# A diffusion-transformer block: fewer dummy matmuls among the first modulation columns, two normalisations moved between scalings, and one K pair moved behind the second chunk's columns

## The chip, the cores and the metric

The kernel runs on one core of one Trainium2 chip. The metric is device time in microseconds (us) of one execution. A run is one execution; times of several runs are given as a median. The profile is one traced execution, whose own span (first to last instruction) is about 2 us shorter than the time.

## The reference

```python
B, N, D = (2, 256, 1152)
mod = (_silu(c) @ w_mod).reshape(B, 6, 1, D)
shift_a, scale_a, gate_a, shift_m, scale_m, gate_m = [mod[:, i] for i in range(6)]
h = _layernorm(x, axis=-1) * (1 + scale_a) + shift_a
qkv = (h @ wqkv).reshape(B, N, 3, H, Dh)
# ... attention, output projection, MLP (cut)
```

Only the opening matters here: layer norm of x, the modulation columns `scale_a` (a matrix-vector product with `w_mod`), the scaling, and the K projection of the scaled activations. (K is computed without `shift_a`, which only adds the same amount to all scores of a query.)

## The kernel before

The kernel writes its instructions down as units, and a small scheduler sets their order on each engine. TensorE (PE) keeps the written order; `S.first` fixes the first part of the order on DVE (VectorE) and ACT (ScalarE). The opening works like this:

- The four activation tiles (two per batch) are loaded, two at a time. DVE takes the statistics of tiles 1 and 2, ACT of tiles 0 and 3; GpSimd (POOL) raises the variance to the power -1/2, and DVE normalises (`xn_t`).
- TensorE transposes the normalised tiles (`xn_T`), and computes the scale columns in 2-column matmuls (`mod_kt`, 15 to a group), in two chunks: five of the nine column blocks first (`sca`), four later (`scb`). Each group of three K rows of `w_mod` is one load.
- DVE adds one to the columns (`sc1a`), DVE and ACT scale the transposed tiles (`hk_<row>_<batch>`), TensorE multiplies them with the K weights (`k_pair`).
- `warm(n)` issues n dummy matmuls of 512 columns, which nobody reads. They are there to keep the array's clock up.

```python
        def warm(n, tag):
            for i in range(n):
                S.unit("pe", 215.0, "warm_%s_%d" % (tag, i))
                mm(ps32(2), IDENT, Q4B, True, True)
...
        warm(12, "b")
        xn_T(1)
        warm(2, "c")
        for kt in range(0, 3):
            mod_kt(WSC, kt, 0, "sca_%d" % kt, (0, KC))      # group one
        xn_T(0)
        warm(2, "d")
        for kt in range(3, 6):
            mod_kt(WSC, kt, 0, "sca_%d" % kt, (0, KC))      # group two
        warm(3, "e")
        for kt in range(6, 9):
            mod_kt(WSC, kt, 0, "sca_%d" % kt, (0, KC))      # group three
        warm(3, "f")
        sc1a(0, KC)
        for kt in range(KC):
            hk(kt, 0, "act" if kt in (2, 4) else "dve")
        ...
        k_pair(range(KC), 0, 1)
        k_pair(range(KC), 1, 1)
        for kt in range(KT):
            mod_kt(WSC, kt, 0, "scb_%d" % kt, (KC, KT))     # chunk two's columns
        sc1a(KC, KT)
        for kt in range(KC, KT):
            for b in range(2):
                hk(kt, b)
        k_pair(range(KC), 2, 1)
```

## Time and profile before

Three runs took 250.62, 251.05 and 251.10 us, median 251.05 us.

The page of the kernel before, first its span and the busy times of part 1, then the engines' shares of the chain that ended last (part 4):

```profile
span 248.7 us, 4155 instructions
PE 242.5 (98%) x1831; PEld 149.8 (60%) x1831; DVE 69.9 (28%) x179; ACT 63.8 (26%) x129; POOL 19.7 (8%) x33
...
PE 94%; ACT 2%; DMA 1%; DVE 1%; issue 0%
```

TensorE is busy nearly all the time and makes up nearly all of the chain. So the question for each part of the change is how much earlier TensorE gets through the opening. The chain of waits of the kernel before, in order of time (start, length, engine and line; line 722 is the statistics, 744 the normalisation, 681 the transposes, 678 all other matmuls, 774 the addition of one, 783 the scaling, 874 a memset of half a query tile):

```profile
...
7.38 0.47 DVE arena L722
7.84 0.49 DVE arena L744
8.33 0.05 issue
8.38 0.68 PE psum L681 x9
9.06 0.81 PE psum L678 x17
9.87 0.52 PE psum L681 x9
10.39 2.00 PE psum L678 x35
12.39 0.02 issue
12.42 0.18 DVE arena L774
...
12.62 0.36 DVE arena L783
...
13.03 1.92 PE psum L678 x16
...
16.83 5.40 PE psum L678 x75
22.23 0.16 DVE arena L774
22.38 0.11 issue
22.49 0.28 DVE arena L874
...
22.80 0.30 DVE arena L783
...
23.14 38.59 PE psum L678 x312
...
```

Read it from the top. Tile 1's normalisation (7.84) releases the first transposes (8.38). From there to 12.39 TensorE never waits: transposes, columns and dummies follow each other. The addition and the first scaling (12.42 to 12.98) release K at 13.03. At 22.23 the chain leaves TensorE again for DVE: addition, memset, first scaling of chunk two. TensorE stood 0.31 us there; chunk two's K starts at 23.14.

A summary of the opening, from successive starts of matmuls in the trace and from its landing records (when the last of 16 engines reported a load):

| before | us |
|---|---|
| first activation tiles landed (x) | 4.37 |
| first transposes | 8.38 |
| group one: weights landed / started | 8.45 / 9.32 |
| group two | 9.71 / 10.66 |
| group three (m): weights landed / started | 10.99 / 11.71 |
| K of batch 0 started | 13.03 |
| chunk two's K started | 23.14 |

### The profile page before, as it was taken

Reading aid. Unit: us, or ns where it says so; the run is one execution under the profiler, and the core shown is the slowest. Engines: PE = TensorE matmul, PEld = TensorE weight load, DVE = VectorE, ACT = ScalarE, POOL = GpSimd, SP = SyncE. Lnnn points to the kernel's source line nnn. Section 1 sums busy time; section 2 is a strip of 40 time slices with the busy share of each in tenths; the row PEclk is TensorE's granted clock in tenths of the full one; section 3 lists DMA queues with packets and bytes.
Section 4 is the critical chain, followed back from the end, with each engine's and each line's share of the span. In section 5 each row is a group of like instructions: output and inputs, shape, how many; then the busy total and the mean of one; then the engine's idle time right before and its main releaser. Section 6 shows DMA issues by size and latency. Waiting matters only on the chain.

```text
span 248.7 us, 4155 instructions
## 1 busy us (share of the span) xinstructions
PE 242.5 (98%) x1831; PEld 149.8 (60%) x1831; DVE 69.9 (28%) x179; ACT 63.8 (26%) x129; POOL 19.7 (8%) x33
## 2 busy tenths in 40 slices
PE   7799999999999999999999999999999999999995
PEld 2588864557656856698644444444556665666574
DVE  3543350456412768951000000000011222211112
ACT  5630340334311402985323322233000000000000
POOL 1400000000003258510000000000000000000000
PEclk9999999999999999999999999999999999999999
DMA  6999969999999999999955660000000000000000
GB/s 246 364 375 391 391 216 409 427 419 420 417 388 354 264 367 390 391 392 383 365 171 175 190 188 4 0 0 0 3 16 16 18 16 16 16 18 17 31 18 17
DMA packets 27644, 51.59 MB, mean 207 GB/s; under 512 B 1511, under 2 KB 15591, under 8 KB 26475
## 3 DMA queue, kind: packets, MB, share of 16 engines
q1 hardware_dynamic: 27216, 50.14, 55.7%
q0 software_dynamic: 384, 1.19, 1.5%
q8 instruction: 14, 0.23, 0.4%
q14 instruction: 3, 0.02, 0.0%
q10 hardware_dynamic: 27, 0.00, 0.0%
HBM read 50.14 MB, written 1.19 MB: 206 GB/s over the span
## 4 chain that ended last, share of the span: by engine, by line
PE 94%; ACT 2%; DMA 1%; DVE 1%; issue 0%
PE psum L678 91%; PE psum L681 2%; DMA arena<-in_x_dram 1%; ACT arena L1051 1%; ACT arena L1035 1%; ACT arena L730 1%; ACT arena L731 1%; DVE arena L783 0%; DVE arena L744 0%; DVE arena L722 0%; DVE arena L774 0%; DVE arena L874 0%; DVE arena L1141 0%; DVE arena L732 0%; DVE arena L1142 0%
## 5 line engine op out<-in xcount | busy, mean ns | idle before, releaser
L678 PE MATMUL psum<-arena 128*128 128x384 bf16 (+7 forms) x1724 | 238.7, 306 | 1.7 <-POOL arena L701 1.4
L678 PEld LDWEIGHTS psum<-arena 128*128 128x128 bf16 (+1 forms) x1724 | 144.0, 97 | 91.6 <-issue 3.0
L1141 DVE TENSOR_TENSOR arena<-psum,arena 128x384 f32<-128x384 f32 (+3 forms) x14 | 7.0, 501 | 119.1 <-PE psum L678 119.1
L1061 ACT ACTIVATE arena<-psum 128x512 bf16<-128x512 f32 (+1 forms) x44 | 22.5, 522 | 42.6 <-PE psum L678 42.6
L673 ACT ACTIVATE arena<-psum 128x512 bf16<-128x512 f32 (+7 forms) x29 | 15.4, 553 | 37.3 <-PE psum L678 33.8
L675 DVE CAST arena<-psum 128x512 bf16<-128x512 f32 (+4 forms) x23 | 14.0, 621 | 30.9 <-PE psum L678 30.8
L1030 POOL TENSOR_TENSOR arena<-arena 128x384 f32<-128x384 f32 x12 | 10.9, 911 | 11.2 <-DVE arena L1029 10.1
L722 DVE BATCH_NORM_STATS2 arena<-arena 128x6 f32<-128x384 f32 (+1 forms) x18 | 9.5, 549 | 1.1 <-DMA arena<-in_x_dram 1.0
L681 PE MATMUL psum<-arena 128*128 128x128 bf16 (+2 forms) x107 | 7.8, 209 | 1.5 <-DVE arena L744 1.4
L681 PEld LDWEIGHTS psum<-arena 128*128 128x128 bf16 (+2 forms) x107 | 6.3, 97 | 4.2 <-DVE arena L744 1.9
L1035 ACT ACTIVATE arena<-arena 128x1152 bf16<-128x1152 f32 x4 | 5.4, 1354 | 9.5 <-DVE arena L1034 9.5
L1029 DVE TENSOR_TENSOR arena<-psum,arena 128x384 f32<-128x384 f32 x12 | 6.6, 548 | 3.2 <-PE psum L678 3.2
L1142 DVE TENSOR_TENSOR arena<-arena 128x384 bf16<-128x384 f32 (+3 forms) x14 | 7.0, 501 | 0.5
L1051 ACT ACTIVATE arena<-psum,arena 128x128 bf16<-128x128 bf16 x16 | 6.1, 460 | 3.2 <-PE psum L681 2.5
L659 POOL DMA_DIRECT2D dit_scratch<-arena x2 | 1.2, 628 | 62.9 <-DVE arena L675 62.9
L1048 DVE TENSOR_SCALAR arena<-psum,arena 128x128 bf16<-128x128 bf16 x20 | 5.5, 336 | 2.0 <-PE psum L681 1.8
L926 ACT ACTIVATE arena<-psum,arena 128x256 bf16<-128x256 f32 x8 | 3.7, 470 | 6.9 <-PE psum L678 5.4
L726 POOL TENSOR_TENSOR arena<-arena 128x1 f32<-128x1 f32 x6 | 3.3, 551 | 8.3 <-DVE arena L725 8.3
L889 ACT ACTIVATE arena<-arena 128x256 bf16<-128x256 bf16 x6 | 2.5, 495 | 4.3 <-DVE arena L883 4.3
L783 DVE TENSOR_SCALAR arena<-psum,arena 128x256 bf16<-128x256 bf16 x7 | 2.3, 348 | 3.6 <-PE psum L681 2.3
L922 DVE TENSOR_REDUCE arena<-psum 128x2 f32<-128x512 f32 x4 | 2.8, 690 | 1.5 <-PE psum L678 1.5
L930 DVE TENSOR_TENSOR arena<-arena 128x512 bf16<-128x512 bf16 x4 | 2.8, 688 | 0.1
(37 smaller groups left out, 31.0 us busy)
## 6 DMA issues: line engine op xcount, KB each, us to landing
arena<-in_w_mod_dram SPq DMA_DIRECT2D x3, 3456.0 KB, 26.2
arena<-in_w_fc_dram SPq DMA_DIRECT2D x9, 1152.0 KB, 9.9
arena<-in_w_fc_dram SPq DMA_DIRECT2D x4, 2592.0 KB, 20.5
arena<-in_wqkv_dram SPq DMA_DIRECT2D x18, 288.0 KB, 9.0
arena<-in_w_mod_dram SPq DMA_DIRECT2D x3, 864.0 KB, 12.6
arena<-in_wqkv_dram SPq DMA_DIRECT2D x1, 2592.0 KB, 9.8
arena<-in_wo_dram SPq DMA_DIRECT2D x1, 2592.0 KB, 40.1
arena<-in_w_mod_dram SPq DMA_DIRECT2D x3, 480.0 KB, 7.6
```

The lines of the kernel that those rows point to most:

```text
L673: act(c_act(n), lambda e: e.activation(out=dst, in_=src, func=ACTF.Copy), [src], [dst], name)
L675: dve(c_dve_psum16(n) if psum16 else c_dve_psum32(n), lambda e: e.tensor_copy(dst, src), [src], [dst], name)
L678: S.instr(lambda e: e.matmul(o, lhsT=l, rhs=r, start=st, stop=sp, **kw), reads=[l, r], writes=[o])
L681: S.instr(lambda e: e.transpose(o, i_, idn), reads=[i_, idn], writes=[o])
L722: dve(550, lambda e, s=s, o=o: e.bn_stats(out=o, in_=s), [s], [o], "bn_%s_%d" % (tag, ci))
L1029: dve(550, lambda e, o=o, ga=ga, x1c=x1c: e.tensor_tensor(out=x1c, in0=o, in1=ga, op=ALU.mult), [o, ga], [x1c], "wo_t1_%d_%d" % (t, ci))
L1030: S.op("pool", 930, lambda e, xs=xs, x1c=x1c: e.tensor_tensor(out=x1c, in0=x1c, in1=xs, op=ALU.add), reads=[x1c, xs], writes=[x1c], name=" ...
L1035: act(1344, lambda e: e.activation(out=xn2, in_=x1, func=ACTF.Identity, scale=rs, bias=nm), [x1, rs, nm], [xn2], "xn2_%d" % t)
L1051: act(440, lambda e, o=o, dst=dst, s1=s1, s2=s2: e.activation(out=dst, in_=o, func=ACTF.Identity, scale=s1, bias=s2), [o, s1, s2], [dst], ...
L1061: act(c_act(ntok), lambda e: e.activation(out=dst, in_=o, func=ACTF.Gelu_apprx_tanh), [o], [dst], "gelu_%d_%d" % (f, tok0))
L1141: dve(c_dve_psum32(w), lambda e, o=o, gm=gm, t1=t1: e.tensor_tensor(out=t1, in0=o, in1=gm, op=ALU.mult), [o, gm], [t1], "fc2_t1_%d_%d" % ( ...
L1142: dve(c_dve_32(w), lambda e, t1=t1, x1c=x1c, ost=ost: e.tensor_tensor(out=ost, in0=t1, in1=x1c, op=ALU.add), [t1, x1c], [ost], "fc2_out_%d ...
```

## The change

The intent is to shorten the opening: fewer dummies in TensorE's way, statistics and normalisations moved into DVE's idle spots, and more K work to hide chunk two's scaling behind. (In this diff, loop bodies are shortened.)

```diff
-        warm(12, "b")
+        warm(14, "b")
         xn_T(1)
-        warm(2, "c")
         for kt in range(0, 3): mod_kt(...)      # group one
         xn_T(0)
-        warm(2, "d")
         for kt in range(3, 6): mod_kt(...)      # group two
-        warm(3, "e")
+        warm(2, "c")
         for kt in range(6, 9): mod_kt(...)      # group three
-        warm(3, "f")
+        warm(2, "d")
         sc1a(0, KC)
 ...
         k_pair(range(KC), 0, 1)
-        k_pair(range(KC), 1, 1)
         for kt in range(KT): mod_kt(...)        # chunk two's columns
         sc1a(KC, KT)
         for kt in range(KC, KT): ...            # hk
+        k_pair(range(KC), 1, 1)
         k_pair(range(KC), 2, 1)
 ...
   S.first["dve"]: (cut to the two places that change)
-  "veps_ln1_1", "nvar_ln1_0", "veps_ln1_0", "bn_ln1_2_0", "xn_1"
+  "veps_ln1_1", "bn_ln1_2_0", "nvar_ln1_0", "veps_ln1_0", "xn_1"
-  "hk_0_0", "hk_1_0", "xn_2", "hk_3_0", "xn_3", "hk_0_1"
+  "hk_0_0", "xn_2", "hk_1_0", "xn_3", "hk_3_0", "z4a", "hk_0_1"
```

The last line also moves `z4a`, the memset that stood in the chain at 22.49.

## The prediction

> **What bounds the kernel now.** TensorE: 242.5 of 248.7 us busy (page, part 1), 94% of the chain that ended last (part 4). Starts of successive matmuls in the trace: at 256 columns every 109 ns, at 512 every 216, at 2 every 26.7. This is the warm spacing in the Trainium skill, "TensorE: Matmul & The Clock Gate", Back-to-back issue gap (N/2.4 + 2.5 ns; about 25 ns at small N); the trace agrees. After 25 us only about 0.65 us of the stream lies outside such spacing, so what the first 23 us give up reaches the end, unless a DMA takes it.
>
> **The head before (timeline, us from the span's start).** First transposes 8.38, behind normalisation of tile 1 (7.76 to 8.32). The three groups of chunk one's modulation columns start at 9.32, 10.65 and 11.70; their weights landed at 8.45, 9.71 and 10.99. The last group is late only because dummies stand before it: 2+2+3 = 7 x 0.216 = 1.5 us. Three more hide under the addition of one (12.42) and the first scaling (to 12.97). K of batch 0 starts at 13.03. Chunk two's columns end near 21.9; one K pair (1.09 us) cannot cover addition, z4a memset (0.27) and first scaling (to 23.08): TensorE stands 0.31 us, and the chain goes through DVE. Chunk two's K starts at 23.14.
>
> **The change, costed.**
> 1. Statistics of tile 2 fill DVE's wait (0.63 us) for ACT: tile 1 is normalised about 0.4 us sooner, transposes at about 7.9. Two more opening dummies (0.43) fall in idle time: free. The early start is not critical, because:
> 2. Dummies ahead of group three fall from 7 to 2, but it cannot start before its weights land, 10.99. Expected start 11.03 instead of 11.70: **-0.67 us**. From there to K takes 1.32 us as before (columns 0.40; wait, addition, first scaling 0.93; two dummies hide as three did). K starts at 12.36. The rest of the 1.5 us becomes a DMA wait.
> 3. Normalisations (0.57 each) between scalings: second scaling ends near 13.06, needed 13.23; fourth near 13.95, needed near 14.3. Both hold: 0.
> 4. Chunk two's columns one pair earlier: two pairs (2.18 us) cover addition and scaling (about 0.85), and the memset leaves that path: **-0.31 us**. Chunk two's modulation weights (last 18.08) and K weights (19.67 on) are in time.
>
> Sum -0.98 us: chunk two's K starts at 22.16. Later loads follow TensorE's release of buffers and shift along, with microseconds to spare.
>
> **Predicted time** 250.1 us (251.05 - 0.98, rounded), 8 in 10 between 249.5 and 250.7. Faster by over 2%: 1%; within 2%: 98%; slower by over 2%: 1%.
>
> **What would show it.** Timeline: group three at 11.0, released by a DMA; K at 12.4; no DVE piece in the chain before chunk two's K, and that at about 22.2; later stages shifted alike. K at 12.0 or earlier: weights landed earlier, step 2 undersized; at 12.7: something else binds.
>
> **What would make it wrong.** (a) The clock. The first nine or so dummies come every 427 ns, then 216 from about 6.1 us: half rate first, as the skill's page tells of the clock gate. Six fewer 512-column dummies between 8 and 13 us leave less work; if the gate closes again, 256-column matmuls would come every 213 ns and cost 1 to 2 us. I give that 10%. (b) Step 3's slack failing: up to 0.3 us back. (c) Weights landing some tenths earlier or later from run to run.

## The result, and the profile after

The changed kernel took 249.57 us (median of four runs, 249.32 to 249.87) against 251.06 us before (four runs). The ratio is 0.9945, 95% interval 0.9927 to 0.9964: about 1.4 us less. Ratios here are the mean time of one kernel's runs over that of the other's of the same rounds, so not quite the ratio of the medians. Within 2%, and inside the predicted range, but the gain is 1.4 us where 0.98 was forecast.

The page of the changed kernel, the same lines:

```profile
span 247.4 us, 4146 instructions
PE 241.7 (98%) x1827; PEld 149.5 (60%) x1827; DVE 69.9 (28%) x179; ACT 63.8 (26%) x129; POOL 19.6 (8%) x33
...
PE 94%; ACT 2%; DMA 2%; DVE 1%; issue 0%
```

The chain of waits of the changed kernel, the same stretch (its line 744, 774, 783 are as before):

```profile
...
7.78 0.50 DVE arena L744
8.28 0.05 issue
8.32 0.68 PE psum L681 x9
9.00 0.38 PE psum L678 x15
9.37 0.65 PE psum L681 x9
10.03 1.35 PE psum L678 x32
11.38 0.02 issue
11.40 0.18 DVE arena L774
...
11.61 0.36 DVE arena L783
...
12.02 1.92 PE psum L678 x16
...
15.81 44.59 PE psum L678 x394
...
```

K starts at 12.02, not at the predicted 12.36. There is no load among these lines: group three was not held by its weights, which the table below shows landed 0.40 us before it started. And from 15.81 on TensorE runs without leaving the chain for 44.59 us; the stop for DVE before chunk two's K is gone. DVE's timeline there (addition, then eight scalings with nothing between):

```profile
20.11 0.17 DVE L774 TENSOR_SCALAR arena<-psum 128x8 f32<-128x8 f32 x1 [1.72 <-PE psum L678]
20.32 1.66 DVE L783 TENSOR_SCALAR arena<-arena 128x256 bf16<-128x256 bf16 x8
```

| landing or start, us | before | after |
|---|---|---|
| first activation tiles landed (x) | 4.37 | 4.77 |
| first transposes | 8.38 | 8.32 |
| group three's weights landed (m) | 10.99 | 10.29 |
| group three started | 11.71 | 10.69 |
| K of batch 0 started | 13.03 | 12.02 |
| wait before chunk two's K | 0.31 | 0.00 |

Two things are odd. The activations landed 0.40 us later in this trace, yet group three's weights landed 0.70 us sooner, though neither version touches these loads. So the weights are only 5.5 us behind the activations here, and 6.6 us in the trace that the prediction was made from.

### The profile page after: what moved, and what is told of

It is laid out like the page before. It is cut to its first block, busy times and chain, and to the rows that moved or that the text cites. A ratio compares the mean times of both kernels' runs of the same rounds, so it can differ in the third digit from the quotient of the medians. Undisturbed runs are those within 1.5% of the kernel's fastest.

```text
span 247.4 us, 4146 instructions
## 1 busy us (share of the span) xinstructions
PE 241.7 (98%) x1827; PEld 149.5 (60%) x1827; DVE 69.9 (28%) x179; ACT 63.8 (26%) x129; POOL 19.6 (8%) x33
## 4 chain that ended last, share of the span: by engine, by line
PE 94%; ACT 2%; DMA 2%; DVE 1%; issue 0%
PE psum L678 92%; PE psum L681 2%; DMA arena<-in_x_dram 2%; ACT arena L1049 1%; ACT arena L1033 1%; ACT arena L731 1%; ACT arena L730 1%; DVE arena L744 0%; DVE arena L783 0%; DVE arena L1139 0%; DVE arena L732 0%; DVE arena L1140 0%; DVE arena L774 0%; DVE arena L734 0%
```

## The experiments

Two explanations of the missing 0.4 us were set against each other. L (landing): the prediction's rule was right, K starts at the later of what TensorE's stream allows and what the third landing allows, but the landing moves from run to run, and the trace before was a late draw. O (order): the new order on DVE, costed at zero, was worth the difference. A third, C, is the clock risk of the prediction. In what follows x and m are the two landings marked so in the tables, in the same run's trace; x+7.6 means 7.6 us after x. Each edit below is against the kernel before (p_...) or the changed one (a_...), five timed rounds each, beside runs of the kernel before on the same chip (medians 251.08, 251.09 and 251.09 us on three chips). All results were correct but the one that is wrong on purpose.

### The dummies alone (p_dummies)

```diff
-        warm(12, "b")
+        warm(14, "b")
         xn_T(1)
-        warm(2, "c")
         for kt in range(0, 3): ...              # group one
         xn_T(0)
-        warm(2, "d")
         for kt in range(3, 6): ...              # group two
-        warm(3, "e")
+        warm(2, "c")
         for kt in range(6, 9): ...              # group three
-        warm(3, "f")
+        warm(2, "d")
```

> The kernel before with the changed dummy matmuls alone (14 at the opening, then 2 and 2). x is the landing of the first activation tile, m the landing of the third group of chunk one's modulation weights, both in this run's trace; K is the start of batch 0's K matmuls (before: x 4.37, m 10.99, K 13.03, which is x+8.66; after: x 4.77, m 10.29, K 12.02, which is x+7.25). Theory L (landing): K starts at the later of x+7.6 (the TensorE stream, with tile 1 normalised late) and m+1.36. With m near 11.0 that gives 12.35 (gain 0.7 us), with m near 10.3 about 12.0 (gain 1.1). Rival O (order): the 0.3 us that the prediction missed came from the new DVE order; then the dummies alone give 0.67 whatever m is. The 0.31 us wait before chunk two's K stays in both.

Measured: 250.14 us, ratio 0.9961 (0.9949 to 0.9973), 1.0 us faster. In the trace x was 4.66 and m 10.77, and K started at 12.24, which is x+7.58 against the expected x+7.6 (m+1.36 would be 12.13). The wait before chunk two's K stayed at 0.31 us. K is thus 1.08 us sooner behind x than x+8.66: the dummies alone are worth more than 0.67 us when the weights land less far behind the activations, as L has it, and O's 0.67 whatever m is falls.

### The DVE order alone (p_order)

```diff
-  "veps_ln1_1", "nvar_ln1_0", "veps_ln1_0", "bn_ln1_2_0", "xn_1"
+  "veps_ln1_1", "bn_ln1_2_0", "nvar_ln1_0", "veps_ln1_0", "xn_1"
-  "hk_0_0", "hk_1_0", "xn_2", "hk_3_0", "xn_3", "hk_0_1"
+  "hk_0_0", "xn_2", "hk_1_0", "xn_3", "hk_3_0", "hk_0_1"
```

> The kernel before with the new DVE order alone (statistics of tile 2 before the variance of tile 0; normalisations of batch 1 between the scalings; the memset left where it was). The prediction called this worth nothing, since a landing would hold group three in the changed kernel; but the TensorE stream of the kernel before has no wait between the first transposes and group three, so alone it should move them all: transposes at x+3.55 instead of x+4.01, K at the later of x+8.2 and m+1.36, a gain of 0.4 to 0.45 us. If the prediction's zero holds also alone, K stays at x+8.66. The 0.31 us wait before chunk two's K stays.

Measured: K at 12.38, which is x+8.20 with x 4.17: 0.46 us sooner than x+8.66, as expected. The time, 250.62 us (ratio 0.9988, 0.9973 to 1.0002), has six runs from 249.98 to 251.48 and does not resolve it; why two of them took over 251 us was not found. The early transposes are thus worth 0.46 us in the kernel before, where TensorE's stream, not a landing, holds K. "The early start is not critical" was said of the changed kernel, whose group three was to wait for its weights; how far it holds there is taken up at the end.

### The memset alone, the pair alone (p_memset, p_pair)

```diff
 (p_memset: S.first of the kernel before)
-  "xn_3", "hk_0_1"
+  "xn_3", "z4a", "hk_0_1"

 (p_pair)
         k_pair(range(KC), 0, 1)
-        k_pair(range(KC), 1, 1)
         for kt in range(KT): ...                # chunk two's columns, addition, scalings
+        k_pair(range(KC), 1, 1)
         k_pair(range(KC), 2, 1)
```

> The kernel before with one move alone: the memset of the query tile's lower half goes from between the addition of one and the scalings of chunk two to before batch 1's scalings. The memset and its hand-over take 0.31 us of the 0.87 us from the addition (22.21) to the first scaled tile (23.08), and TensorE stood 0.31 us there, so the wait before chunk two's K should fall from 0.31 to under 0.03 us and the time by 0.3 us. If the K pair's move is what removes the wait, this alone should leave over 0.15 us of it.

> The kernel before with one move alone: chunk two's modulation columns one K pair earlier, the memset left late. Two pairs (2.18 us) stand against about 1.2 us from the last column to the first scaled tile, so the wait before chunk two's K should be 0 and the time 0.3 us shorter. If memset and pair are both needed, some of the 0.31 us stays here and in the run that moves the memset alone.

Measured: the wait before chunk two's K is 0.00 us in both. The stretch from K's start to the shift columns, which is 18.20 us in both traces of the kernel before, is 17.88 us in both of these and in the changed kernel: 0.32 us less, each time. DVE's timeline without the memset (p_memset), then with it but behind one more pair (p_pair):

```profile
22.13 0.17 DVE L774 TENSOR_SCALAR arena<-psum 128x8 f32<-128x8 f32 x1 [2.81 <-PE psum L678]
22.34 1.66 DVE L783 TENSOR_SCALAR arena<-arena 128x256 bf16<-128x256 bf16 x8
```

```profile
21.55 0.17 DVE L774 TENSOR_SCALAR arena<-psum 128x8 f32<-128x8 f32 x1 [1.72 <-PE psum L678]
21.82 0.27 DVE L874 MEMSET arena<- 64x256 uint32 x1
22.13 1.66 DVE L783 TENSOR_SCALAR arena<-arena 128x256 bf16<-128x256 bf16 x8
```

In the second the memset (line 874) still stands between addition and scaling, and costs nothing. So the prediction's 0.31 us is right, but the change pays for it twice: either edit alone takes the whole wait away. The times, 250.33 us (ratio 0.9976, 0.9964 to 0.9988) and 250.75 us (0.9985, 0.9973 to 0.9997), agree in sign; their difference is no more than the spread that the start of the activations brings (x was 4.28 in one trace and 4.79 in the other).

### Both kernels again (b_again, a_again)

> The kernel before, unchanged, for a second trace: how far the landings differ from run to run. In its first trace the stream of landings paused early (5.78 to 8.45 between the second activation tile and the first modulation weights, 2.7 us for 0.49 MB where the next took 1.3); in the changed kernel's trace the pause stood later (16.5 to 19.05). Theory L: the pause wanders from run to run and is not the change's doing; K here stays at x+8.66 within 0.1 wherever it stands, since the dummies keep TensorE behind the landings. If the pause belongs to the program, it will stand at 5.8 to 8.5 again.

> The changed kernel, unchanged, for a second trace. Theory L: K starts at the later of x+7.25 and m+1.36 of this trace; a pause before m would put K near 12.35, no pause near 12.0. Rival O: K is at x+7.25 whatever m is.

Measured: b_again 250.96 us (ratio 1.0001), a_again 249.52 us (ratio 0.9948, 0.9936 to 0.9960). In b_again K is at x+8.66 again. In a_again x was 4.76 and m 10.86, and K started at 12.21, which is m+1.35 and x+7.46: here the landing did hold it, as the prediction said. Its chain of waits:

```profile
...
2.84 8.02 DMA arena<-in_w_mod_dram
10.90 0.67 PE psum L678 x15
11.60 0.18 DVE arena L774
11.80 0.36 DVE arena L783
12.21 1.92 PE psum L678 x16
...
```

This is the predicted picture: a load of `w_mod` (8.02 us from issue to landing) releases group three at 10.90. Beside it stands the first trace of the same kernel, in which tile 1's normalisation is what the chain goes through. Rival O, K at x+7.25 whatever m is, falls. But O had a part of the truth: p_dummies has the same delay m - x, 6.10 us, and without the new DVE order its K came at x+7.58 against x+7.46 here.

One part of L fell too. The pause in the landings after the second activation tile does not wander: it stood there again in b_again (6.06 to 8.30), and in twelve of all fourteen traces that interval was 1.9 to 2.7 us; it was 1.5 in the other two, the first of the changed kernel being one. Its length is what varies.

### Without the last four dummies, and without the wait for the third landing (a_nodummy, a_nodummy_b, a_bare3)

```diff
 (a_nodummy and a_nodummy_b: the changed kernel)
-        warm(2, "c")
         for kt in range(6, 9): ...              # group three
-        warm(2, "d")

 (a_bare3: that, and group three reads group one's weights; wrong on purpose; edit in short)
-                   W[:, kt, f * 128:(f + 1) * 128]
+                   W[:, kt - 6, f * 128:(f + 1) * 128]      # for kt 6 to 8
```

> The changed kernel without its last four dummies (two before group three, two before K). Theory L: K starts at the later of x+6.82 (0.43 less, the two dummies before group three) and m+1.36; so 0.0 to 0.4 us faster than the changed kernel, none of it where m lands at 11.0. The two dummies before K hide behind the scaling and give nothing. Rival C (clock): dummies between the transposes and K keep the array's clock up; without them 256-column matmuls come every 213 ns for some microseconds and the kernel is 0.5 us or more slower than the changed one.

> The same without dummies, and group three multiplies with group one's weights, which have landed: its result is wrong on purpose, and only the wait for the third landing is gone. Theory L: K starts at the later of x+6.82 and the second group's landing +1.76, never later than without dummies; if m was what held that run, K here is up to 0.5 us earlier, in a trace where m lands at 11.0. If m never binds, no difference.

> The changed kernel without its last four dummies again, for a trace of the slower kind: five of its six runs took 251.0 to 251.3 us at a granted clock of 0.992 to 0.993, and the traced one 249.25 at 0.998. Rival C (clock) now expects a trace with one stretch in which 256-column matmuls come every 213 ns instead of 109. From the clock, 0.7% of 249 us, i.e. about 3.4 us at half rate, costing about 1.7 us. If the slower runs come instead from a late landing, the trace shows 109 ns throughout and a wait of 1.5 us or more.

Measured, start of K: a_nodummy 11.90 (m 10.55, so m+1.35), a_nodummy_b 12.08 (m 10.73, m+1.35): the landing binds, as L says. In a_bare3 (relative error 0.054, as intended) it was 11.72 with x 4.79 and m 10.44: 0.08 us earlier than m+1.36, and group three started at 10.28, before m, so the third landing no longer held it, but 0.11 us later than the expected x+6.82. There DVE still had statistics of batch 1 in its queue when the columns were done, so a third limit seems to have come up just behind the other two (read from DVE's timeline, not tested).

Times: a_nodummy 251.07 us (249.25 to 251.28), a_nodummy_b 250.42 us (249.41 to 251.39), a_bare3 249.45 us (249.09 to 250.69). These are in two heaps, and the granted clock tells them apart: every run over 250.5 us had a clock of 0.991 to 0.993, every other 0.998 or above. The low heap holds 8 of the 12 runs without dummies and 2 of the 6 of a_bare3. (A clock of 0.998 comes from the end of the program: in p_dummies the clock falls at 246.99 us of 247.9, after the last matmul.) None of the low runs here was traced, since the profile is of the first run; the next experiment caught one.

### Other places for the dummies (a_hidden2, a_front2, a_hidden4)

```diff
 (a_hidden2: the changed kernel)
-        warm(2, "c")
 (a_front2: the changed kernel)
-        warm(2, "d")
 (a_hidden4: the changed kernel)
-        warm(2, "c")
-        warm(2, "d")
+        warm(4, "d")
```

> The changed kernel without the two dummies before group three, keeping the two before K. Start of K as without dummies: the later of x+6.82 and m+1.36, so 0 to 0.4 us sooner than the changed kernel. If the last two dummies hold the clock, all runs stand at 0.998 or above and 249.2 to 249.6 us; if dummies between the transposes are needed, some runs fall to 0.993 and 251.

> The changed kernel with the two dummies before group three, without the two before K. Start of K as in the changed kernel (the later of x+7.25 and m+1.36), about 249.5 us if the clock holds; runs at 0.993 and 251 if the two before K are what holds it.

> The candidate that should beat both: no dummies before group three, four (0.86 us) in the 0.93 us between the last column and K, where TensorE waits for the addition and the first scaling anyway. K at the later of x+6.82 and m+1.36, clock 0.998 or above in all runs: 249.1 to 249.6 us, 0 to 0.4 us faster than the changed kernel. If the clock falls nevertheless, the place of the dummies and not their number holds it.

Measured: a_hidden2 249.49 us, one of six runs at clock 0.991 with 251.55 us; a_front2 249.87 us, two of six at 0.992 and 0.993 with 250.99 and 251.29; a_hidden4 249.73 us, one of six at 0.993 with 251.52. One or two low runs of six do not tell these from the changed kernel's none of nine; the eight of twelve above do. So whether the number of dummies or their place holds the clock stays open. The traced run of a_hidden2 was the low one. TensorE's timeline in it:

```profile
9.64 0.55 PE L678 MATMUL psum<-arena 128*128 128x2 bf16 x15
11.28 1.00 PE L678 MATMUL psum<-arena 128*128 128x2 bf16 x16 [1.09 <-DMA arena<-in_w_mod_dram]
12.59 1.31 PE L678 MATMUL psum<-arena 128*128 128x256 bf16 x8 [0.31 <-DVE arena L783]
```

The weights landed as late as 11.24 in this run (m is x+6.83, the latest of all fourteen traces), and without the two dummies before group three TensorE had nothing to do: group three waited 1.09 us by this view. Stretches of the same trace, with each engine's busy time and number of instructions (PE, PEld, DVE, ACT, POOL), then PEclk, the granted clock, then the share and rate of the DMA:

```profile
6.00:8.00 2.00, 1.96 (x9) 0.68 (x8) 1.67 (x6) 2.00 (x4) 1.06 (x2) 1.00 0.94 326
8.00:10.00 2.00, 2.00 (x47) 1.78 (x47) 1.62 (x4) 1.68 (x6) 0.31 (x1) 1.00 1.00 330
10.00:12.00 2.00, 0.83 (x24) 0.61 (x21) 0.58 (x5) 0.79 (x2) 1.06 (x2) 1.00 1.03 372
12.00:14.00 2.00, 1.69 (x11) 1.13 (x11) 1.91 (x6) 0.69 (x2) 0.00 (x0) 0.81 1.05 401
14.00:16.00 2.00, 2.00 (x14) 1.54 (x13) 0.23 (x2) 0.15 (x1) 0.00 (x0) 0.50 1.09 365
16.00:18.00 2.00, 2.00 (x25) 1.84 (x23) 0.21 (x1) 0.00 (x0) 0.00 (x0) 0.84 1.08 366
```

By the trace's clock records the clock fell to half at 13.23 and stayed there for 3.41 us, exactly two such intervals after it had opened at 6.40. (At the end of the other thirteen traces it falls 70 or 71 such intervals, 238.93 or 242.35 us, after it opened.) Successive 256-column matmuls came every 213 ns instead of 109, and the stretch from K to the shift columns took 19.54 us instead of 17.88: 1.66 us lost. A half-rate stretch of 3.41 us in 249 us is a mean clock of 0.993, and 0.991 with the fall at the end of this trace; the untraced low runs show 0.991 to 0.993. Theory C is shown in this trace, and for the others argued from the clock alone.

How little work was too little? I summed, from the trace, the columns streamed at 2.4 GHz (transposes counted) in the second 3.41 us interval after the clock opened. In this trace they fill 25%. In the thirteen others they fill 51% to 83%, and none closed; in the first interval 45% or more did not close it either. That sets this failure apart from the other openings, but it gives no limit: in b_again the interval from 30.78 us, full of 2-column matmuls, comes to 32% by the same sum and the clock held, while at the end of a_nodummy one of 35% was followed by a fall. Nor is it the longest pause: that was 1.23 us here, and the kernel before paused 1.54 us by the same reckoning before its first transposes and kept its clock. What exactly the clock goes by is not shown.

The candidate that should beat both kernels, a_hidden4, does not: its five runs at full clock took 249.33 to 250.02 us, no less than the changed kernel's nine runs (249.32 to 249.87, all at clock 1.0), and one run lost 1.7 us. In its trace K stood at m+1.35 (11.98), where x+7.25 would have given 12.03, so the two dummies it saved before group three were mostly standing in a wait for the weights anyway. No other version was better.

## Why the prediction was right, and what was undersized

| trace | x | m | m - x | K by the rule | K measured |
|---|---|---|---|---|---|
| before | 4.37 | 10.99 | 6.62 | 13.03 (x+8.66) | 13.03 |
| b_again | 4.66 | 10.99 | 6.33 | 13.32 (x+8.66) | 13.32 |
| after | 4.77 | 10.29 | 5.53 | 12.02 (x+7.25) | 12.02 |
| a_again | 4.76 | 10.86 | 6.10 | 12.22 (m+1.36) | 12.21 |
| p_dummies | 4.66 | 10.77 | 6.10 | 12.26 (x+7.6) | 12.24 |
| p_order | 4.17 | 10.60 | 6.42 | 12.37 (x+8.2) | 12.38 |
| a_nodummy | 4.37 | 10.55 | 6.18 | 11.91 (m+1.36) | 11.90 |
| a_hidden2 | 4.41 | 11.24 | 6.83 | 12.60 (m+1.36) | 12.59 |

(The delay m - x in the other six: p_memset 6.50, p_pair 6.16, a_nodummy_b 5.94, a_bare3 5.65, a_front2 6.05, a_hidden4 5.85.)

The rule "the later of the stream and the third landing" gives K within 0.02 us in thirteen of the fourteen traces (a_bare3 is the exception, by 0.11). Only x+8.66 and x+7.25 were read from the traces they are checked on; the rest was written before the runs. Of these two, x+8.66 was checked again in b_again and p_pair, but x+7.25 is what binds only in the trace it was read from.

Point by point:

- What bounds the kernel: right. TensorE's stream passes the gain of the opening on to the end; the later stages moved as a block (the stretch of 134.79 us that ends the chain starts at 111.09 before and 109.77 after).
- Step 2, the dummies: right in kind, undersized (0.67 us forecast; the traces give about 1.1). The failing term is the difference of two starts of group three, 11.03 (its weights land at 10.99) "instead of 11.70", both taken from one trace as fixed times: the first follows the weights, the second the activations, and both landings move from run to run. The prediction had named the sign itself ("K at 12.0 or earlier: weights landed earlier, step 2 undersized"). With the landing delay m - x of each of the fourteen traces put into the rule, the gain in K's start behind x, x+8.66 less the later of x+7.25 and m+1.36, is 0.47 to 1.41 us, mean 1.09. The trace before had the second longest delay of the fourteen, and from it the same sum gives 0.68. 1.09 and the 0.32 of the second wait make 1.41 us, and 1.38 and 1.31 us were measured (from the ratios 0.9945 and 0.9948). The sum takes the delay to be the same whatever the kernel, which is not shown: the six traces of the kernel before and its edits give 0.94 us, the eight of the changed kernel and its edits 1.20.
- Which landing was off: mostly the activations'. In the thirteen traces without the half-rate stretch, the run's time less K's start is 237.60 to 237.64 us where the second wait stands and 237.31 to 237.37 us where it is gone, so a time tells where K started (an estimate for runs without a trace). The trace before is of a run of 250.66 us with x at 4.37; the median of 251.06 us means K at about 13.4 and x at about 4.8, where group three started at 12.12 in p_pair, not at 11.70. The prediction took the gain seen in a quick run off the median of all runs. Off that run's own 250.66 us, 0.98 gives 249.68, within 0.2 us of the measured 249.57 and 249.52. The weights' 10.99 was off by less: m averages 10.76 over the fourteen traces. So the "late draw" of L was for the larger part an early landing of the activations.
- Step 1, the early transposes: "not critical" was wrong in both traces of the changed kernel: by the rule the early start was worth 0.35 us in the first and about 0.1 us in a_again. In the kernel before they are worth 0.46 us. Inside the change they count only where the weights land under about 6.2 us behind the activations, and then at most 0.35 us (x+7.6 against x+7.25). With x+7.6 in place of x+7.25 the sum over the fourteen delays gives 0.95 us, so about 0.14 of the 1.09 is theirs.
- Step 3, normalisations between scalings: right; no new wait of TensorE appears there.
- Step 4, the second wait: right in size (0.31 predicted, 0.32 measured). What it did not say is that either half of it was enough.
- The clock: its fall did not come in nine runs of the changed kernel, but it was a real risk: with four dummies fewer it came, by the granted clock, in 8 of 12 runs.

Left open: why the landings vary. The delay m - x is shorter where the activations came late: x ran from 4.17 to 4.79 us, and the seven traces with x above 4.7 have delays of 5.53 to 6.16 us, the other seven 6.10 to 6.83. In the trace before, fifteen of the sixteen engines had reported group three's weights at 10.15 us and the last at 10.99; in the first trace after, at 10.25 and 10.29. So the late landing of that trace is one engine behind the rest. What held that engine this early, no view here shows.

## What to carry to other kernels

Before costing the removal of filler work, ask what stands next behind it, and if that is a load, look at its landing in more than one trace: with one trace the gain was read as 0.68 us, over fourteen it averaged 1.09. Compare the traced run's own time with the median from which the gain is to be taken: here they were 0.4 us apart. Write the start of a stage as the later of two or three limits and check it trace by trace; start times within one trace decide what five timed rounds cannot. And dummy matmuls are priced by what they prevent: the ones taken out here were free to remove (no fall of the clock in nine runs), the next four cost 1.7 us in most of the runs without them.

## What the Trainium skill lacked or had wrong

- "TensorE: Matmul & The Clock Gate", Why this matters for your kernels, asks for no idle gaps over about 3 us between bursts. Here the clock fell to half (for 3.41 us, the window that the page's Part 1 gives, agreed) though the longest gap between matmuls was 1.23 us; what was low was the work in the 3.41 us before, 25% of full streaming against 51% to 83% in the thirteen other traces. The page also tells of a kernel whose frequent short idles made the clock go up and down, but it gives no share of work that is enough, and the runs here give none either.
- The same page, Back-to-back issue gap: the isolated formula N/2.4 + 2.5 ns agrees (109 ns at 256 columns, 216 at 512), and 26.7 ns at 2 columns with its floor. Its sustained figure of about 131 ns at 512 columns is not what this kernel's stream shows: 216 ns.
- "DMA: Bandwidth & Descriptors", Why a DMA increments its semaphore by 16 and not by 1, says that the engines finish independently; the runs agree (15 of 16 at 10.15 us, the last at 10.99). No page says how far that moves an early landing from run to run: in fourteen traces with the same loads the activations landed at 4.17 to 4.79 us, and group three's weights 5.5 to 6.8 us behind them.
